# Batch 0 of an attention and FFN kernel: values loaded before queries, queries in two pairs, buffer clearing moved

## Chip, cores, metric

One core of one Trainium2 chip. The metric is the device time of the whole kernel in microseconds (us), median of several runs. "Span" in the profile is some 1.8 to 1.9 us shorter than this time (259.6 against 261.4 for the profiled run of the kernel before), because it runs from the first to the last instruction.

## The reference, cut

```python
# attention: batch 8, heads 8, sequence 576, head size 64
r   = maximum(x, 0);  phi(x) = concat(r * cos_w, r * sin_w)    # 64 -> 128 features, weights by position
kv  = einsum('bhsf,bhsd->bhfd', phi(k), v);   z = sum(phi(k), axis=2)
x   = einsum('bhsf,bhfd->bhsd', phi(q), kv) / (phi(q) . z + 1e-6)
# FFN on x as 4608 tokens of 512
out = ((x @ w1) * (x @ w2)) @ w3 @ w_out       # the kernel multiplies w3 @ w_out once
```

## The kernel before

The tokens go through the FFN in nine tiles of 512. The attention of later batches is spread in "slots" between the FFN products. Only batch 0 has nothing to hide behind: its attention is a prologue. These are its parts (cuts marked).

```python
    load_first(nc.sync, k0, k)              # keys, fp32, 1 MB, on the SyncE queue
    load_first4(nc.sync, k0, k)
    load_first(nc.gpsimd, q0, q)            # queries, 512 KB as bf16, GpSimd queue
    ...
    idle_mms(34)                            # products of zeros: keep TensorE's clock up
    cosv, sinv = _trig_tables(nc, const)    # position table, on VectorE
    load_first(nc.gpsimd, v0, v)            # values
    load_first4(nc.gpsimd, v0, v)
    make_identity(nc, identb[:])
    for i in range(2):                      # two sets of feature buffers
        ... memset ones column of va, and the unused half of va, kp, qp (chunk 4)
    ... loads of w1, w2, wout, w3, batch 1 and 2, all on the GpSimd queue

    def features(b, dst, src, c):           # cosine half on VectorE, sine half on ScalarE
    def kv_first():                         # key-value products: heads 0-3 over all chunks, then 4-7
    def q_tr(b, c):                         # 8 transposes of query features, copied to qpT
    def num(b, c):                          # 8 products, then on VectorE: den, reciprocal, xblk
    def x_tr(b, c):                         # 4 transposes of xblk, copied to xT on ScalarE

    # the prologue
    for c in range(NCH): prep_k(0, c)
    for c in range(4):   prep_q(0, c)
    for c in range(3):   q_tr(0, c)
    idle_mms(1)
    for c in range(NCH): prep_v(0, c)
    q_tr(0, 3, evac=False)[1]()             # copied by ScalarE
    kv_first()
    idle_mms(1); num(0, 0); num(0, 1); idle_mms(3); num(0, 2); x_tr(0, 0)
    idle_mms(2); num(0, 3); x_tr(0, 1)
    first.close()                           # its PSUM banks become the FFN accumulators
    ps_ffn = ...
    # tile 0: the first products in quarters of 128 tokens; x_tr(0, 2), x_tr(0, 3) in slots 0 and 1
            for quarter in range(4):
                for i in range(4):
                    products(acc[i], (w1b, w2b)[i % 2], i // 2, ts(quarter, 128))
                    ...
                yield
```

Of the kernel before, what the change touches and what calls it, by code (L numbers as in the profile page):

```python
# [10 lines left out]
FP32 = mybir.dt.float32  # L11
BF16 = mybir.dt.bfloat16
I32 = mybir.dt.int32
ALU = mybir.AluOpType
ACTF = mybir.ActivationFunctionType

P = 128
H, S, D = 8, 576, 64
F = 2 * D
NCH = 5  # L20
# [48 lines left out]
def kernel(  # L69
# [11 lines left out]
    nc = tc.nc  # L81
# [32 lines left out]
                                in_=src[b, :, 320:S, :].rearrange("h (p j) d -> p h (j d)", j=4))  # L114
            raw[b, name] = t

    def load_first(eng, t, src):
        eng.dma_start(out=t[:, :, 0:4, :].rearrange("p h j d -> p h (j d)"),  # L118
                      in_=src[0, :, 0:512, :].rearrange("h (p j) d -> p h (j d)", j=4))

    def load_first4(eng, t, src):
        eng.dma_start(out=t[0:64, :, 4, :], in_=src[0, :, 512:S, :].rearrange("h p d -> p h d"))
# [14 lines left out]
    v0 = raw[0, "v"] = ld.tile([P, H, NCH, D], BF16, name="vs")  # L137
    load_first(nc.sync, k0, k)
    load_first4(nc.sync, k0, k)
    load_first(nc.gpsimd, q0, q)  # L140
    zeros = const.tile([P, 512], BF16, name="zeros")
    nc.vector.memset(zeros[:], 0.0)
    tiny = const.tile([P, 1], FP32, name="tiny")
    nc.scalar.activation(out=tiny[:], in_=zeros[:, 0:1], func=ACTF.Relu, scale=1.0, bias=0.0)

    unread = ps_first.tile([P, 512], FP32, name="unread")

    def idle_mms(n):

        for _ in range(n):  # L150
            nc.tensor.matmul(unread[:, :], lhsT=zeros[:, 0:128], rhs=zeros[:], start=True, stop=True)

    idle_mms(34)
    cosv, sinv = _trig_tables(nc, const)
    identb = const.tile([P, P], BF16, name="identb")
    load_first(nc.gpsimd, v0, v)
    load_first4(nc.gpsimd, v0, v)
    make_identity(nc, identb[:])

    va_bufs, kp_bufs, qp_bufs = [], [], []  # L160
    for i in range(2):
        va = const.tile([P, NCH, H, D + 2], BF16, name=f"va{i}")
        nc.vector.memset(va[:, :, :, D:D + 1], 1.0)
        nc.vector.memset(va[64:128, 4, :, 0:D], 0.0)
        va_bufs.append(va)
        for name, bufs in (("kp", kp_bufs), ("qp", qp_bufs)):
            fp = const.tile([P, NCH, H, F], BF16, name=f"{name}{i}")
            nc.vector.memset(fp[64:128, 4, :, :], 0.0)  # L168
            bufs.append(fp)
    for c0, n in ((0, 256), (256, 256), (512, 512)):  # L170
        nc.gpsimd.dma_start(out=w1b[:, :, ds(c0, n)], in_=w1v[:, :, ds(c0, n)])
        nc.gpsimd.dma_start(out=w2b[:, :, ds(c0, n)], in_=w2v[:, :, ds(c0, n)])
        if c0 == 0:
            load_first4(nc.gpsimd, q0, q)
# [69 lines left out]
    def prep_q(b, c):  # L244
        features(b, feat_of(b)[1], raw[b, "q"], c)
        if c in dma_q(b):
            R = ROWS[c]
            nc.sync.dma_start_transpose(out=att_of(b)["qpT"][:, :, ds(columns_of(b, c), R)],
                                        in_=feat[b][1][:R, c].rearrange("p h f -> p (h f)"))
# [21 lines left out]
    def kv_first():  # L271

        kp, qp, va = feat[0]
        kvs = sm.tile([P, H, D + 1], BF16, name="kvs", bufs=2)
        kva = ps_first.tile([P, 512], FP32, name="kva")
        kvb = ps_att.tile([P, 2, 512], FP32, name="pnum")
        for half, kvt in enumerate((kva[:, :], kvb[:, 0, :])):
            for c in range(NCH):
                for i in range(4):
                    nc.tensor.matmul(kvt[:, ds(i * 65, 65)], lhsT=kp[:, c, 4 * half + i, :],  # L280
                                     rhs=va[:, c, 4 * half + i, 0:D + 1],
                                     start=(c == 0 and i == 0), stop=(c == NCH - 1 and i == 3))
            dst, src = kvs[:, 4 * half:4 * half + 4, :], kvt[:, 0:260]
            if half == 0:
                nc.scalar.copy(out=dst, in_=src)
            else:
                nc.vector.tensor_copy(out=dst, in_=src)
        att_of(0)["kvs"] = kvs

    def q_tr(b, c, evac=True):  # L290
        R = ROWS[c]
        qp = feat[b][1]
        pst = ps_tr.tile([P, 8, 128], BF16, name="pst")
        for h in range(H):
            nc.tensor.transpose(pst[:, h, :], qp[:, c, h, :], identb[:])  # L295
        dst, src = att_of(b)["qpT"][:, :, ds(columns_of(b, c), R)], pst[:, :, 0:R]
        on_vector = lambda: nc.vector.tensor_copy(out=dst, in_=src)  # L297
        on_scalar = lambda: nc.scalar.copy(out=dst, in_=src)
        if evac:
            on_vector()  # L300
        return on_vector, on_scalar
# [81 lines left out]
    def ffn_groups(t):  # L383
        x = xT[t]
        abT = fsb.tile([P, 8, 512], BF16, name="abT", bufs=2)

        def products(out_ps, w, jc, tok):
            for kc in range(4):
                nc.tensor.matmul(out_ps[:, tok], lhsT=w[:, kc, ts(jc, 128)], rhs=x[:, kc, tok],  # L389
                                 start=(kc == 0), stop=(kc == 3))  # L390

        def to_abT(jc, aT, bT):
            asb = fsb.tile([P, 512], BF16, name="asb")
            nc.scalar.copy(out=asb[:], in_=aT[:, :])
            nc.vector.tensor_mul(out=abT[:, jc, :], in0=asb[:], in1=bT[:, :])

        if t == 0:
            acc = [ps_ffn.tile([P, 512], FP32, name="ffnps") for _ in range(4)]
            for quarter in range(4):
                for i in range(4):  # L400
                    products(acc[i], (w1b, w2b)[i % 2], i // 2, ts(quarter, 128))
                    if i % 2 == 1 and quarter == 3:
                        to_abT(i // 2, acc[i - 1], acc[i])
                yield
        for jc in range(2 if t == 0 else 0, 8):
            aT = ps_ffn.tile([P, 512], FP32, name="ffnps")
            products(aT, w1b, jc, slice(0, 512))
            asb = fsb.tile([P, 512], BF16, name="asb")
            nc.scalar.copy(out=asb[:], in_=aT[:, :])  # L409
            yield  # L410
            bT = ps_ffn.tile([P, 512], FP32, name="ffnps")
            products(bT, w2b, jc, slice(0, 512))
            nc.vector.tensor_mul(out=abT[:, jc, :], in0=asb[:], in1=bT[:, :])  # L413
            yield
        for ms in range(3 if t == NT - 1 else 4):
            ops = ps_ffn.tile([P, 512], FP32, name="ffnps")
            for jc in range(8):
                nc.tensor.matmul(ops[:, :], lhsT=abT[:, jc, ts(ms, 128)], rhs=w34b[:, jc, :],  # L418
                                 start=(jc == 0), stop=(jc == 7))
                if jc == 3:  # L420
                    yield
            if ms % 2 == 0:
                osb = fsb.tile([P, 2, 512], FP32, name="osb", bufs=2)
            nc.scalar.copy(out=osb[:, ms % 2, :], in_=ops[:, :])  # L424
            if t == NT - 1:
                store(nc.sync, osb[:, ms % 2:ms % 2 + 1, :], 4 * t + ms, 1)
            elif ms % 2 == 1:
                store(nc.gpsimd, osb[:, :, :], 4 * t + ms - 1, 2)
            yield
        if t == NT - 1:  # L430
            for half in range(2):
                cols = ts(half, 256)
                ops = ps_ffn.tile([P, 512], FP32, name="ffnps")
                for jc in range(8):
                    nc.tensor.matmul(ops[:, 0:256], lhsT=abT[:, jc, ts(3, 128)],
                                     rhs=w34b[:, jc, cols], start=(jc == 0), stop=(jc == 7))
                nc.scalar.copy(out=osb[:, 1, cols], in_=ops[:, 0:256])
                store((nc.sync, nc.scalar), osb[:, 1:2, :], 4 * t + 3, 1, cols)
                yield
# [9 lines left out]

    for c in range(NCH):  # L450
        prep_k(0, c)
    for c in range(4):
        prep_q(0, c)
    for c in range(3):
        q_tr(0, c)
    idle_mms(1)
    for c in range(NCH):
        prep_v(0, c)
    q_tr(0, 3, evac=False)[1]()
    kv_first()  # L460
    idle_mms(1)
    num(0, 0)
    num(0, 1)
    idle_mms(3)
    num(0, 2)
    x_tr(0, 0)
    idle_mms(2)
    num(0, 3)
    x_tr(0, 1)
    first.close()  # L470
    ps_ffn = ctx.enter_context(tc.tile_pool(name="ps_ffn", bufs=4, space=bass.MemoryType.PSUM))

    for t in range(NT):
        slots = [[] for _ in range(24)]
        if t == 0:
            slots[0].append(lambda: x_tr(0, 2))
            slots[1].append(lambda: x_tr(0, 3))
            slots[1].append(lambda: prep_q(0, 4))
# [63 lines left out]
```

## Time and profile before

| | kernel before |
|---|---|
| time, median (lowest to highest of 3 runs) | 261.54 us (261.39 to 261.55) |
| granted TensorE clock, mean | 0.998 |
| first FFN product (first of w1, 128 columns) | 21.29 us |
| first full FFN product (512 columns) | 25.52 us |
| last products of the kernel start | 253.18 us |

The three marks are read from the timeline of TensorE and from the chain of waits. They cut the span into the prologue, the quarter products of tile 0, and the rest. In the rest TensorE is dense, so it should always last the same: 253.18 - 25.52 = 227.66 us. If a kernel shows more there, a new wait has come up. In profile lines, PE is TensorE, PEld its weight loads, DVE VectorE, ACT ScalarE and POOL GpSimd. The tiles are kf, qs and vs (keys, queries and values as loaded), kp and qp (their features), va (values as copied for the products), kva and pnum (key-value products and numerators, in PSUM, the memory that TensorE writes), kvs (the former, copied), qpT (transposed query features), xblk (a normalised block, 128 rows of attention output) and xT (its transpose). L numbers are lines of that kernel's own source, "A<-B" means that A is written from B, and "[4.94 <-DMA kf]" that the engine sat idle 4.94 us until DMA finished kf.

### The profile page before, as it was taken

How to read it: one execution, taken by the hardware profiler on the slowest of the kernel's cores; microseconds unless marked ns; L12 is line 12 of the kernel's file. 1: busy time of each engine (PE TensorE's matmuls, PEld its weight loads, DVE VectorE, ACT ScalarE, POOL GpSimd, SP SyncE). 2: the span in 40 equal slices, each digit the busy share in tenths (PEclk: the TensorE clock that was granted, in tenths of full speed). 3: DMA queues.
4: the chain of work that ended last, by engine and by line, in shares of the span. 5: the costliest groups of instructions: out<-in, count | busy, mean ns of one | idle time of the engine just before them, and what ended most of it. 6: DMA issues, size and time to landing. Idle time of an engine off the chain costs nothing.

```text
span 259.6 us, 5067 instructions
## 1 busy us (share of the span) xinstructions
PE 250.6 (97%) x1961; PEld 134.9 (52%) x1961; DVE 147.2 (57%) x345; ACT 127.2 (49%) x218; POOL 83.3 (32%) x143
## 2 busy tenths in 40 slices
PE   8789999999999999999999999999999999999992
PEld 2367455666555556445544654464455444444442
DVE  5975656478699627844873587178616613413310
ACT  2826327637955554654655555645533233323322
POOL 7462245340591276047404910520050031012000
PEclk9999999999999999999999999999999999999999
DMA  7999999999399889977998999825590252014015
GB/s 192 188 196 207 210 200 204 199 199 195 96 180 174 145 184 179 196 134 153 190 166 182 155 197 129 184 81 107 107 202 13 40 115 90 0 32 132 1 42 121
DMA packets 65928, 37.10 MB, mean 143 GB/s; under 512 B 33520, under 2 KB 62448, under 8 KB 65904
## 3 DMA queue, kind: packets, MB, share of 16 engines
q0 software_dynamic: 33392, 27.20, 63.7%
q1 hardware_dynamic: 32352, 9.44, 20.2%
q8 instruction: 15, 0.25, 0.4%
q10 hardware_dynamic: 160, 0.13, 0.2%
q14 instruction: 9, 0.07, 0.1%
HBM read 38.80 MB, written 9.44 MB: 186 GB/s over the span
## 4 chain that ended last, share of the span: by engine, by line
PE 90%; DVE 5%; issue 1%; POOL 1%; ACT 1%; ACTq 0%; POOLq 0%
PE ffnps L389 48%; PE ffnps L418 23%; PE ffnps L205 5%; PE pst L295 4%; PE pnum L313 4%; PE pnum L262 3%; PE pst L193 1%; DVE kp L236 1%; DVE xblk L320 1%; PE pst L342 1%; DVE qpT L297 1%; PE kva L280 0%; DVE qp L236 0%; POOL qs L118 0%; DVE qp L168 0%
## 5 line engine op out<-in xcount | busy, mean ns | idle before, releaser
L413 DVE TENSOR_TENSOR abT<-asb,ffnps 128x512 bf16<-128x512 bf16 x70 | 47.8, 683 | 69.3 <-PE ffnps L389 66.7
L389 PE MATMUL ffnps<-xT,w1b 128*128 128x512 bf16 (+1 forms) x312 | 74.9, 362 | 0.5 <-DVE den L317 0.5
L389 PE MATMUL ffnps<-xT,w2b 128*128 128x512 bf16 (+1 forms) x312 | 74.9, 362 | 0.0
L409 ACT CAST asb<-ffnps 128x512 bf16<-128x512 f32 x70 | 41.0, 586 | 64.9 <-PE ffnps L389 57.9
L418 PE MATMUL ffnps<-w34b,abT 128*128 128x512 bf16 x280 | 63.7, 379 | 0.0
L381 POOL DMA_DIRECT2D out_dram<-osb x42 | 22.3, 537 | 122.4 <-ACT osb L424 122.3
L389 PEld LDWEIGHTS <-w1b 128*128 128x128 bf16 x312 | 28.0, 98 | 28.2 <-issue 0.8
L418 PEld LDWEIGHTS <-abT 128*128 128x128 bf16 x280 | 26.7, 98 | 30.2
L389 PEld LDWEIGHTS <-w2b 128*128 128x128 bf16 x312 | 26.9, 98 | 23.9
L424 ACT COPY osb<-ffnps 128x512 f32<-128x512 f32 x35 | 20.5, 585 | 36.6 <-PE ffnps L418 36.6
L238 ACT ACTIVATE qp<-qs,sinv 128x512 bf16<-128x512 bf16 (+1 forms) x40 | 28.2, 721 | 0.0
L320 DVE TENSOR_TENSOR xblk<-pnum,den 128x512 bf16<-128x512 f32 (+1 forms) x38 | 26.3, 691 | 1.3
L238 ACT ACTIVATE kp<-ks,sinv 128x512 bf16<-128x512 bf16 (+1 forms) x35 | 24.7, 722 | 0.0
L313 PEld LDWEIGHTS <-qpT 128*128 128x128 bf16 x320 | 15.1, 98 | 9.3 <-DVE xblk L320 1.5
L254 POOL COPY va<-vs 128x512 bf16<-128x512 bf16 (+1 forms) x30 | 18.6, 644 | 0.0
L236 DVE TENSOR_SCALAR qp<-qs,cosv 128x512 bf16<-128x512 bf16 (+1 forms) x40 | 18.1, 468 | 0.0
L297 DVE COPY qpT<-pst 128x1024 bf16<-128x1024 bf16 (+1 forms) x23 | 14.4, 628 | 4.7 <-PE pst L295 4.2
L295 PEld LDWEIGHTS <-qp 128*128 128x128 bf16 x192 | 12.5, 98 | 7.2 <-ACT qp L238 1.9
L295 PE MATMUL pst<-identb,qp 128*128 128x128 bf16 x192 | 14.5, 219 | 1.8 <-DVE qp L236 1.4
L313 PE MATMUL pnum<-kvs,qpT 128*128 128x65 bf16 x304 | 16.0, 194 | 0.0
L205 PE MATMUL ffnps<-woutb,w3T 128*128 128x512 bf16 x64 | 15.8, 379 | 0.0
L262 PEld LDWEIGHTS <-kp 128*128 128x128 bf16 x280 | 12.9, 98 | 5.4
(73 smaller groups left out, 174.7 us busy)
## 6 DMA issues: line engine op xcount, KB each, us to landing
out_dram<-osb POOLq DMA_DIRECT2D x16, 256.0 KB, 3.9
out_dram<-osb POOLq DMA_DIRECT2D x24, 128.0 KB, 3.0
ks<-in_k_dram POOLq DMA_DIRECT2D x7, 320.0 KB, 5.9
vs<-in_v_dram POOLq DMA_DIRECT2D x7, 320.0 KB, 8.0
qs<-in_q_dram POOLq DMA_DIRECT2D x7, 320.0 KB, 6.5
w3b<-in_moe_w_dram POOLq DMA_DIRECT2D x8, 256.0 KB, 15.0
ks<-in_k_dram POOLq DMA_DIRECT2D x7, 256.0 KB, 6.7
vs<-in_v_dram POOLq DMA_DIRECT2D x7, 256.0 KB, 9.7
```

Source lines behind the costliest of these rows:

```text
L205: nc.tensor.matmul(acc[:, :], lhsT=w3T[:, lc, :], rhs=woutb[:, lc, :], start=(lc == 0), stop=(lc == 7))
L236: nc.vector.tensor_scalar(out=dst[:R, c, :, 0:D], in0=src[:R, :, c, :], scalar1=0.0, scalar2=cosv[:R, at:at + 1], op0=ALU.max, op1=ALU.mult)
L238: nc.scalar.activation(out=dst[:R, c, :, D:F], in_=src[:R, :, c, :], func=ACTF.Relu, scale=sinv[:R, at:at + 1], bias=0.0)
L262: nc.tensor.matmul(kvt[:, h // 4, ds((h % 4) * 65, 65)], lhsT=kp[:, c, h, :], rhs=va[:, c, h, 0:D + 1], start=(i == 0 and h % 4 == 0), sto ...
L295: nc.tensor.transpose(pst[:, h, :], qp[:, c, h, :], identb[:])
L313: nc.tensor.matmul(nt[:, h // 4, ds((h % 4) * 65, 65)], lhsT=qpT[:, h, ds(at, 128)], rhs=kvs[:, h, :], start=True, stop=True)
L320: nc.vector.tensor_tensor(out=xblk[rows], in0=n4[:, :, :, 0:D], in1=den[rows].unsqueeze(3).to_broadcast([R, 2, 4, D]), op=ALU.mult)
L381: on.dma_start(out=rows[:, :, cols], in_=osb[64 * i:64 * i + rows.shape[0], :, cols])
L389: nc.tensor.matmul(out_ps[:, tok], lhsT=w[:, kc, ts(jc, 128)], rhs=x[:, kc, tok], start=(kc == 0), stop=(kc == 3))
L409: nc.scalar.copy(out=asb[:], in_=aT[:, :])
L413: nc.vector.tensor_mul(out=abT[:, jc, :], in0=asb[:], in1=bT[:, :])
L418: nc.tensor.matmul(ops[:, :], lhsT=abT[:, jc, ts(ms, 128)], rhs=w34b[:, jc, :], start=(jc == 0), stop=(jc == 7))
```

## The change

The intent: clear the buffers when VectorE has nothing to do, compute the key-value products while the queries are still in flight, split the queries so that the first two chunks go ahead, and put the fourth numerator among the first FFN products.

```diff
-    def load_first(eng, t, src):
+    def load_first(eng, t, src, c0=0, n=4):          # chunks c0 to c0+n
...
-    load_first(nc.gpsimd, q0, q)
+    load_first(nc.gpsimd, v0, v)
     zeros = ...; nc.vector.memset(zeros[:], 0.0)
+    def feature_buffers(i): ...                       # the clearing, as before
+    feature_buffers(0)
...
-    idle_mms(34)
+    idle_mms(28)
     cosv, sinv = _trig_tables(nc, const)
-    load_first(nc.gpsimd, v0, v)
     load_first4(nc.gpsimd, v0, v)
+    load_first(nc.gpsimd, q0, q, 0, 2)
     make_identity(nc, identb[:])
-    for i in range(2): ...                            # the clearing of both sets
+    load_first(nc.gpsimd, q0, q, 2, 2)
...                                                    # kv_first: all heads of a chunk, chunk by chunk
     for c in range(NCH): prep_k(0, c)
-    for c in range(4): prep_q(0, c)
-    for c in range(3): q_tr(0, c)
-    idle_mms(1)
     for c in range(NCH): prep_v(0, c)
-    q_tr(0, 3, evac=False)[1]()
     kv_first()
+    for c in range(2): prep_q(0, c)
+    idle_mms(2); q_tr(0, 0); q_tr(0, 1)
+    for c in range(2, 4): prep_q(0, c)
     idle_mms(1)
     num(0, 0)
+    q_tr(0, 2, evac=False)[1]()
+    idle_mms(1)
+    q_tr3 = q_tr(0, 3, evac=False)[1]
     num(0, 1)
-    idle_mms(3); num(0, 2); x_tr(0, 0); idle_mms(2); num(0, 3); x_tr(0, 1)
+    idle_mms(2); x_tr(0, 0); q_tr3(); num(0, 2); x_tr(0, 1)
+    feature_buffers(1)
     first.close()
...
-            for quarter in range(4): ...
+            for group in (((0, 0),), ((0, 1), (1, 0)), ((1, 1), (0, 2), (1, 2)), ((0, 3), (1, 3))):
...
         if t == 0:
+            slots[0].append(lambda: num(0, 3))
```

More of the change, by code (lines that the diff above doesn't have):

```diff
@@ L115, in load @@
             raw[b, name] = t
-    def load_first(eng, t, src):
-        eng.dma_start(out=t[:, :, 0:4, :].rearrange("p h j d -> p h (j d)"),
-                      in_=src[0, :, 0:512, :].rearrange("h (p j) d -> p h (j d)", j=4))
+    def load_first(eng, t, src, c0=0, n=4):
+        rows = src[0, :, 0:512, :].rearrange("h (p j) d -> p h j d", j=4)
+        eng.dma_start(out=t[:, :, c0:c0 + n, :].rearrange("p h j d -> p h (j d)"),
+                      in_=rows[:, :, c0:c0 + n, :].rearrange("p h j d -> p h (j d)"))
     def load_first4(eng, t, src):
@@ L139, with feature_buffers @@
     load_first4(nc.sync, k0, k)
-    load_first(nc.gpsimd, q0, q)
+    load_first(nc.gpsimd, v0, v)
     zeros = const.tile([P, 512], BF16, name="zeros")
     nc.vector.memset(zeros[:], 0.0)
-    tiny = const.tile([P, 1], FP32, name="tiny")
-    nc.scalar.activation(out=tiny[:], in_=zeros[:, 0:1], func=ACTF.Relu, scale=1.0, bias=0.0)
-    unread = ps_first.tile([P, 512], FP32, name="unread")
-    def idle_mms(n):
-        for _ in range(n):
-            nc.tensor.matmul(unread[:, :], lhsT=zeros[:, 0:128], rhs=zeros[:], start=True, stop=True)
-    idle_mms(34)
-    cosv, sinv = _trig_tables(nc, const)
-    identb = const.tile([P, P], BF16, name="identb")
-    load_first(nc.gpsimd, v0, v)
-    load_first4(nc.gpsimd, v0, v)
-    make_identity(nc, identb[:])
     va_bufs, kp_bufs, qp_bufs = [], [], []
-    for i in range(2):
+    def feature_buffers(i):
         va = const.tile([P, NCH, H, D + 2], BF16, name=f"va{i}")
@@ L169, with idle_mms @@
             bufs.append(fp)
+    feature_buffers(0)
+    tiny = const.tile([P, 1], FP32, name="tiny")
+    nc.scalar.activation(out=tiny[:], in_=zeros[:, 0:1], func=ACTF.Relu, scale=1.0, bias=0.0)
+    unread = ps_first.tile([P, 512], FP32, name="unread")
+    kva = ps_first.tile([P, 512], FP32, name="kva")
+    def idle_mms(n):
+        for _ in range(n):
+            nc.tensor.matmul(unread[:, :], lhsT=zeros[:, 0:128], rhs=zeros[:], start=True, stop=True)
+    idle_mms(28)
+    cosv, sinv = _trig_tables(nc, const)
+    identb = const.tile([P, P], BF16, name="identb")
+    load_first4(nc.gpsimd, v0, v)
+    load_first(nc.gpsimd, q0, q, 0, 2)
+    make_identity(nc, identb[:])
+    load_first(nc.gpsimd, q0, q, 2, 2)
     for c0, n in ((0, 256), (256, 256), (512, 512)):
@@ L274, in kv_first @@
         kvs = sm.tile([P, H, D + 1], BF16, name="kvs", bufs=2)
-        kva = ps_first.tile([P, 512], FP32, name="kva")
         kvb = ps_att.tile([P, 2, 512], FP32, name="pnum")
-        for half, kvt in enumerate((kva[:, :], kvb[:, 0, :])):
-            for c in range(NCH):
-                for i in range(4):
-                    nc.tensor.matmul(kvt[:, ds(i * 65, 65)], lhsT=kp[:, c, 4 * half + i, :],
-                                     rhs=va[:, c, 4 * half + i, 0:D + 1],
-                                     start=(c == 0 and i == 0), stop=(c == NCH - 1 and i == 3))
-            dst, src = kvs[:, 4 * half:4 * half + 4, :], kvt[:, 0:260]
-            if half == 0:
-                nc.scalar.copy(out=dst, in_=src)
-            else:
-                nc.vector.tensor_copy(out=dst, in_=src)
+        halves = (kva[:, :], kvb[:, 0, :])
+        for c in range(NCH):
+            for h in range(H):
+                nc.tensor.matmul(halves[h // 4][:, ds((h % 4) * 65, 65)], lhsT=kp[:, c, h, :],
+                                 rhs=va[:, c, h, 0:D + 1], start=(c == 0 and h % 4 == 0),
+                                 stop=(c == NCH - 1 and h % 4 == 3))
+        nc.scalar.copy(out=kvs[:, 0:4, :], in_=halves[0][:, 0:260])
+        nc.vector.tensor_copy(out=kvs[:, 4:8, :], in_=halves[1][:, 0:260])
         att_of(0)["kvs"] = kvs
@@ L398, in ffn_groups @@
             acc = [ps_ffn.tile([P, 512], FP32, name="ffnps") for _ in range(4)]
-            for quarter in range(4):
-                for i in range(4):
-                    products(acc[i], (w1b, w2b)[i % 2], i // 2, ts(quarter, 128))
-                    if i % 2 == 1 and quarter == 3:
-                        to_abT(i // 2, acc[i - 1], acc[i])
+            for group in (((0, 0),), ((0, 1), (1, 0)), ((1, 1), (0, 2), (1, 2)), ((0, 3), (1, 3))):
+                for jc, quarter in group:
+                    products(acc[2 * jc], w1b, jc, ts(quarter, 128))
+                    products(acc[2 * jc + 1], w2b, jc, ts(quarter, 128))
+                    if quarter == 3:
+                        to_abT(jc, acc[2 * jc], acc[2 * jc + 1])
                 yield
@@ L451 @@
         prep_k(0, c)
-    for c in range(4):
-        prep_q(0, c)
-    for c in range(3):
-        q_tr(0, c)
-    idle_mms(1)
     for c in range(NCH):
         prep_v(0, c)
-    q_tr(0, 3, evac=False)[1]()
     kv_first()
+    for c in range(2):
+        prep_q(0, c)
+    idle_mms(2)
+    q_tr(0, 0)
+    q_tr(0, 1)
+    for c in range(2, 4):
+        prep_q(0, c)
     idle_mms(1)
     num(0, 0)
+    q_tr(0, 2, evac=False)[1]()
+    idle_mms(1)
+    q_tr3 = q_tr(0, 3, evac=False)[1]
     num(0, 1)
-    idle_mms(3)
+    idle_mms(2)
+    x_tr(0, 0)
+    q_tr3()
     num(0, 2)
-    x_tr(0, 0)
-    idle_mms(2)
-    num(0, 3)
     x_tr(0, 1)
+    feature_buffers(1)
     first.close()
```

## The prediction

> **What bounds the kernel now.** I read the views in this order: the busy time of each engine in stretches of the span, the chain of work that ended last, the timeline of the first 28 us, and the DMA issues with their times to landing.
>
> The stretches say that there are two regimes.
>
> ```profile
> core 0: us, PE busy (x) PEld busy (x) DVE busy (x) ACT busy (x) POOL busy (x), PEclk, DMA share, GB/s
> 0.00:11.00 11.00, 9.78 (x34) 3.80 (x34) 7.17 (x27) 5.31 (x9) 8.37 (x19) 1.00 1.07 190
> 11.00:21.30 10.30, 7.28 (x120) 5.52 (x121) 8.56 (x27) 4.21 (x7) 4.49 (x7) 1.00 1.46 196
> 21.30:32.00 10.70, 10.62 (x117) 7.29 (x118) 5.58 (x12) 4.80 (x10) 2.62 (x4) 1.00 1.20 209
> ...
> 60.00:235.00 175.00, 175.00 (x1333) 91.93 (x1331) 103.59 (x236) 91.82 (x158) 55.37 (x94) 1.00 0.78 134
> ```
>
> The reader is to see the first number after the comma. From 21.3 us on TensorE is busy without a gap (10.62 of 10.70, then 175.00 of 175.00), and the change does not touch the work there apart from its first 5 us. Before 21.3 us its 34 early matmuls are multiplications of zeros, and VectorE is the engine that is nearly full (8.56 of 10.30). So only the prologue can give time, and what it gives must survive 200 us of dense TensorE work: the start of the dense work moves the end one for one, unless a load becomes late.
>
> The chain of waits names the path through the prologue.
>
> ```profile
> 9.80 2.19 DVE kp L236 x5
> 11.99 1.05 DVE qp L236 x4
> ...
> 13.04 0.70 DVE qpT L297
> ...
> 15.12 0.21 DVE va L254
> ...
> 15.38 1.09 PE kva L280 x20
> 16.46 0.65 PE pnum L280 x20
> ...
> 20.46 0.69 DVE xblk L320
> 21.15 0.08 DVE den L317
> 21.23 0.06 issue
> 21.29 1.05 PE ffnps L389 x16
> ```
>
> It is VectorE almost throughout. The first FFN product at 21.29 waits until the third normalised block (20.46 + 0.69 = 21.15) has been read out of its PSUM banks, because the FFN accumulators take those banks.
>
> ```profile
> 7.17 3.17 ACT L238 ACTIVATE kp<-kf,sinv 128x512 bf16<-128x512 f32 x5 [4.94 <-DMA kf<-in_k_dram]
> 8.76 0.48 DVE L168 MEMSET kp<- 64x512 uint32 x1
> 9.80 2.19 DVE L236 TENSOR_SCALAR kp<-kf,cosv 128x512 bf16<-128x512 f32 x5
> 10.03 0.96 POOL L171 DMA_DIRECT2D w1b<-in_moe_w_dram  x1 [1.27 <-DMA qs<-in_q_dram]
> 12.97 0.74 POOL L172 DMA_DIRECT2D w2b<-in_moe_w_dram  x1 [1.98 <-DMA vs<-in_v_dram]
> 15.09 1.01 ACT L298 COPY qpT<-pst 128x1024 bf16<-128x1024 bf16 x1 [2.30 <-PE pst L295]
> ```
>
> In this timeline the keys are there at 7.17 (ScalarE starts), yet VectorE starts on them only at 9.80: it is clearing buffers from 6.52 to 9.79. The bracketed releasers give the loads: the first 512 KB on the GpSimd queue (queries) has landed by 10.03, the second (values) by 12.97; by issue plus time to landing they are 9.8 and 12.7, and the 64 KB of values after them 13.2.
>
> **What the Trainium skill says.** First, "DMA: Bandwidth & Descriptors", section Specifications, puts the least transfer for line rate at 512 B. The split query load has pieces of 512 B in memory and 256 B on chip, against 1 KB and 512 B. The trace only partly agrees that small pieces hurt: 64 KB of values in 256 B source pieces took 13.2 - 12.7 = 0.5 us for 512 pieces, while 512 KB took about 2.9 us for 1024 pieces of 1 KB, so bytes count more than pieces. Second, "TensorE: Matmul & The Clock Gate", section "Wait — 56ns, not 53.3ns?", has warm matmuls of 128 columns 55.6 ns apart; 16 of L389 take 0.89 us in the chain, 55.6 ns each, so it agrees. Third, "VectorE: DVE Perf Modes", section "Why PSUM operands drop a tier", explains why reading PSUM stays slow: the normalisation of 512 elements takes 0.69 us here and no reordering shortens it.
>
> **The change part by part.**
>
> *Memsets.* The first buffer set is cleared while VectorE waits for the position table (idle 1.81 us before 2.95); its four memsets take about 1.5 us (6.52 to 8.06), so the table still starts near 2.95 and ends near 6.4. The second set goes behind the third normalised block. VectorE can start the keys at about 7.2 and end at 7.2 + 2.2 = 9.4. Worth 9.80 - 7.2 = 2.6 us, if what follows is there.
>
> *Values first.* They take the queries' place and land at 9.8 to 10.0, their last chunk by 10.5. Copies to the value buffer: 10.0 to 11.1 (1.08 for five). The 40 key-value products follow chunk by chunk; the last 20 in the trace took 0.65, 33 ns each, so eight take 0.26 against 0.21 for a copy: from 10.3 to about 11.7. Both halves are then copied at once, 0.43, to 12.2. Before, this was 17.57.
>
> *Queries in two pairs.* Two points give a line: 512 pieces of 256 B in 0.5 us, 512 of 1 KB in 1.45; so 512 of 512 B about 0.85, a pair of chunks (1024 pieces) 1.7. They land at about 12.2 and 13.9 (estimate). VectorE makes the cosine features of the first pair 12.2 to 12.75; ScalarE, at 0.635 each, 12.2 to 13.5, and of the second pair 13.9 to 15.2. The first transpose starts at 12.9; from its start to the copy was 0.64 (12.40 to 13.04), so the two copies of qpT (0.69 each) run 13.5 to 14.9, then cosine features of the second pair to 15.45. First normalisation (0.18 + 0.21 + 0.69 with gaps is 1.08): 15.45 to 16.5. Transposes of chunks 2 and 3: 15.2 to 16.3; second numerator to 16.7; second normalisation 16.75 to 17.8. Now ScalarE copies chunk 2 of qpT (1.01) 15.85 to 16.85, the first xT (0.59) 17.3 to 17.9, chunk 3 17.9 to 18.9. Third numerator 17.2 to 17.6, third normalisation 17.8 to 18.85. First FFN product: **18.9**, against 21.29, so 2.4 us earlier.
>
> *What is paid back.* In the order of the built program the first FFN product still waits for the third normalised block, so the reordering does not lift that wait. The fourth numerator, done before the FFN until now, comes inside it: 0.45. Its normalisation stands behind the second set of memsets, 1.55, so block four is ready at 18.85 + 1.55 + 1.08 = 21.45. TensorE meanwhile does eight products (0.45), numerator (0.45), a transpose (0.22), sixteen products (0.9): it reaches the fourth transpose at 20.95 and stalls 0.5. Then 0.22, 24 products (1.35), 16 products (0.9): ends at 24.0. Before, the 64 quarter products ended at 25.26. Gain 25.26 - 24.0 = **1.25 us**.
>
> *Zero products.* 28 instead of 34 at the start, four fewer later: none on the path; the 28 end at 10.98 - 6 x 0.215 = 9.7, before the values.
>
> *Downstream.* Loads do not come earlier when TensorE does. Issue plus time to landing: second part of batch 1's queries 46.7, first used about 47.45; its values 42.3, used 43.8; weights w3 block 6 47.6, used 49.76. A shift of 1.25 turns only the queries into a wait, of about 0.5, on ScalarE, which idles over 1 us soon after (49.28); TensorE needs them at 51.06. So all 1.25 us reach the end: 261.5 - 1.25 = 260.2, 0.5%.
>
> **The rivals.** (1) Pieces set the query load: at 2.9 us a pair as for 1024 pieces now, the pairs land at 13.3 and 16.2, ScalarE ends features at 17.5, the third block moves to 20.8 and the gain becomes a loss of about 0.7: 262.2. Against it stands the 0.5 us of the 256 B pieces. (2) ScalarE sets the end instead of VectorE: it alternates between 1.01 copies of qpT and xT copies, and the fourth numerator needs the last one (18.9 above, just in time). With 0.5 us of slip there: 260.7. (3) The stall behind the memsets is hidden, because TensorE arrives later than I reckon or numerators slip: no stall, 259.7. (4) Sparser TensorE work from 9.7 to 19 lets its clock drop; the granted clock is 1.00 through the old gaps of 1.4 us, and I count about 7 us of work in 9.2, as dense as before. If it drops, half a microsecond to one is lost. (5) Batch 1's loads, pushed by the longer query load, bind at 45 to 50 us and cap the gain near 1 us.
>
> **Range and chances.** Centre 260.2. Half a microsecond either way comes from the stall and ScalarE, the tail upward from rival 1: 259.2 to 261.4 eight times in ten. Faster by over 2% would need 5.2 us, over twice the whole advance at the first FFN product; slower by over 2% would need the loads to come 7 us late. Chances: faster 0.01, same 0.98, slower 0.01.
>
> **What would show it.** In the changed timeline: keys on VectorE at about 7.2; values copied from about 10.0; kvs by 12.2; first pair of query features released by its load near 12.2, second near 13.9; first FFN product near 18.9, released by the third block; an idle of about 0.5 on TensorE before the fourth transpose, released by the fourth block; quarter products over by 24.0; no new idle of TensorE after. I am wrong if the second pair lands after 15, if the first FFN product is later than 20, or if TensorE shows waits between 35 and 60 us.

## The result, and the profile after

The changed kernel takes 259.91 us (259.70 to 260.16, 4 runs) against 261.48 (4 runs) of the kernel before. The ratio is 0.9941, 95% interval 0.9923 to 0.9958. All runs are fast (none is over 1.5% above the fastest of its kernel). A ratio here is the mean time of one kernel's fast runs over the mean of the other's in the same rounds, so it is not quite the ratio of the medians quoted.

Busy time by stretch, kernel after, the same columns as in the prediction:

```profile
11.00:21.30 10.30, 7.47 (x117) 5.73 (x114) 8.54 (x24) 6.49 (x10) 4.63 (x8) 1.00 1.47 197
21.30:32.00 10.70, 10.62 (x97) 6.38 (x96) 4.88 (x10) 5.00 (x9) 2.62 (x4) 1.00 1.20 208
...
60.00:235.00 175.00, 175.00 (x1327) 91.62 (x1326) 102.81 (x234) 91.29 (x157) 56.45 (x96) 1.00 0.79 137
```

The dense regime is unchanged: 175.00 of 175.00, and the same clock. What moved is how early it begins. The chain of waits of the kernel after:

```profile
1.28 8.12 DMA vs<-in_v_dram
...
9.43 0.31 DVE va L260
...
11.15 0.38 ACT kvs L288
11.53 0.63 ACT qp L244
...
12.86 1.30 DVE qpT L299 x2
...
17.61 0.69 DVE xblk L322
...
19.44 0.48 DVE qp L154
...
20.40 0.70 DVE xblk L322
21.10 0.05 issue
21.15 0.40 PE pst L344 x4
```

Read it from the top. The chain no longer starts on VectorE but with the load of the values. From there it goes through the value copies, the first query feature on ScalarE and the query copies to the third block (17.61). Then comes what is new: the clearing of the second set (19.44 is its last piece) and the fourth block, on which the fourth transpose waits. The timeline has the same with the idle times:

```profile
6.76 2.29 DVE L242 TENSOR_SCALAR kp<-kf,cosv 128x512 bf16<-128x512 f32 x5 [0.56 <-DMA kf<-in_k_dram]
11.56 0.74 POOL L178 DMA_DIRECT2D w2b<-in_moe_w_dram  x1 [0.39 <-DMA qs<-in_q_dram]
12.98 0.88 POOL L181 DMA_DIRECT2D woutb<-in_moe_w_out_dram  x1 [0.68 <-DMA qs<-in_q_dram]
18.45 0.38 PE L391 MATMUL ffnps<-xT,w1b 128*128 128x128 bf16 x4 [0.64 <-DVE xblk L322]
21.15 0.40 PE L344 MATMUL pst<-identb,xblk 128*128 128x128 bf16 x4 [0.72 <-DVE xblk L322]
```

VectorE now waits for the keys (0.56 us) where it was clearing buffers before. The first pair of queries has landed by 11.56 and the second by 12.98. TensorE stalls 0.72 us at 21.15.

The three marks of every kernel, each from its profiled run:

| kernel | median us | ratio to before | first FFN product | to first full product | from there to the last products |
|---|---|---|---|---|---|
| before | 261.4 to 261.5 | 1 | 21.29 | 4.23 | 227.66 |
| after | 259.91 | 0.9941 | 18.45 | 5.38 | 227.66 |
| after, once more | 260.08 | 0.9944 | 18.70 | 5.38 | 227.66 |
| clearing moved, nothing else | 260.35 | 0.9958 | 20.35 | 4.22 | 227.66 |
| all but the clearing | 262.24 | 1.0032 | 21.65 | 4.76 | 227.67 |
| the same, 42 zero products | 261.99 | 1.0026 | 21.44 | 4.76 | 227.67 |
| the same, 39 zero products | 261.49 | 0.9998 | 21.03 | 4.77 | 227.67 |
| queries whole | 261.10 | 0.9984 | 19.65 | 5.38 | 227.65 |
| second set cleared before the keys | 259.79 | 0.9939 | 19.21 | 4.76 | 227.67 |
| second set cleared in slot 5 | 259.89 | 0.9944 | 18.60 | 4.77 | 228.28 |
| old quarter order | 259.58 | 0.9929 | 18.84 | 4.94 | 227.64 |
| second set cleared in slot 10 | 259.49 | 0.9925 | 18.81 | 4.77 | 227.76 |
| combined | 259.56 | 0.9929 | 18.45 | 4.76 | 228.19 |
| combined, w3 block ahead | 260.41 | 0.9956 | 18.69 | 4.77 | 228.86 |

The change gains 21.29 - 18.45 = 2.84 us up to the first FFN product, gives 5.38 - 4.23 = 1.15 back in the quarter products, and nothing after: 1.69 us between the profiled runs. The two right-hand columns repeat to 0.02 us where the code is the same, so they are the ones to compare.

The first mark does not repeat so well. Five of these kernels have the prologue of the change unaltered up to this mark (after, once more, slot 5, slot 10, old quarter order), and their first mark lies between 18.45 and 18.84; the profiled run of the change is the fastest of its four. The spread begins where the key-value products start, at 9.78 to 10.14. They need three things that come within half a microsecond of each other, and each came last in one of these runs: the copied values in the changed kernel (their load landed at 9.40), ScalarE's half of the key features in the slot 10 run (until 10.10), and the end of the 28 zero products in the run with the old quarter order (10.07). Zero products start 0.43 us apart at first and 0.22 apart later. The switch came between 3.7 and 7.0 us, differently from run to run, and the clock column shows 1.00 all the while (its record begins only about there). So a number of zero products does not fix when they end.

### The profile page after: what moved, and what is told of

Its sections match the earlier page's. It is cut to its first block, busy times and chain, and to the rows that moved or that the text cites. A ratio compares the mean times of both kernels' runs of the same rounds, so it can differ in the third digit from the quotient of the medians.

```text
span 257.9 us, 5056 instructions
## 1 busy us (share of the span) xinstructions
PE 248.3 (96%) x1954; PEld 134.0 (52%) x1954; DVE 147.0 (57%) x344; ACT 128.3 (50%) x219; POOL 84.3 (33%) x144
## 2 busy tenths in 40 slices
DMA packets 66968, 37.10 MB, mean 144 GB/s; under 512 B 35584, under 2 KB 63488, under 8 KB 66944
## 4 chain that ended last, share of the span: by engine, by line
PE 91%; DMA 3%; DVE 2%; ACT 1%; issue 1%; ACTq 0%; POOLq 0%
PE ffnps L391 47%; PE ffnps L421 23%; PE ffnps L211 5%; PE pst L297 4%; PE pnum L315 4%; PE pnum L268 3%; DMA vs<-in_v_dram 3%; PE pst L199 1%; DVE xblk L322 1%; PE pst L344 1%; DVE qpT L299 1%; PE ffnps L438 0%; PE kva L285 0%; ACT osb L440 0%; DVE den L320 0%
## 5 line engine op out<-in xcount | busy, mean ns | idle before, releaser
L391 PEld LDWEIGHTS <-w2b 128*128 128x128 bf16 x312 | 26.9, 97 | 23.9
L299 DVE COPY qpT<-pst 128x1024 bf16<-128x1024 bf16 (+1 forms) x22 | 13.7, 626 | 5.0 <-PE pst L297 4.7
```

The lines of the kernel that those rows point to most:

```text
L391: nc.tensor.matmul(out_ps[:, tok], lhsT=w[:, kc, ts(jc, 128)], rhs=x[:, kc, tok], start=(kc == 0), stop=(kc == 3))
```

## The experiments

All kernels gave correct results. All but the first start from the changed kernel; all were run in five rounds with the kernel before.

### 1. The clearing alone

```diff
 # kernel before
+    feature_buffers(0)                  # after the memset of zeros
...
-    for i in range(2): ...              # both sets, between position table and keys
...
     x_tr(0, 1)
+    feature_buffers(1)                  # behind the fourth block
     first.close()
```

> The kernel before with nothing but the buffer clearing moved: first set while VectorE waits for the position table, second set behind the fourth normalised block. Loads, order of work and quarter products as before. My working: keys on VectorE at 7.2 instead of 9.8, query features held by their load at 9.8, the transposed-query copies 11.6 to 13.7, the value copies 13.7 to 14.8 instead of 15.0 to 16.1 (values land at 13.2), so 1.3 us earlier from there on, 260.2. Rival A (the clearing is the whole of the change, the load order adds nothing): as the changed kernel, 259.9. Rival B (the value load at 12.7 to 13.2 holds the old order, so early keys give nothing): 261.3 or more.

Measured 260.35 us, ratio 0.9958 (0.9945 to 0.9970). The first FFN product comes at 20.35, 0.94 us earlier; nothing is given back. Neither rival holds: the clearing alone brings 1.0 us, about two thirds of the change's gain. It lies 0.15 above my number. The value copies ran from 13.64 as reckoned, but took 1.53 us instead of 1.08, because the second of the five took 0.73 and the others 0.28; why it did is not shown.

### 2. All but the clearing

```diff
-    feature_buffers(0)
...
     make_identity(nc, identb[:])
+    for i in range(2): feature_buffers(i)      # as in the kernel before
...
-    feature_buffers(1)
```

> The changed kernel with both sets cleared where the kernel before cleared them, ahead of the keys; loads, order and quarter products stay changed. My working: keys end at about 12, value copies 12 to 13.1 although the values landed at 9.4, the first FFN product 2.4 us later than in the changed kernel (20.9), but the stall before the fourth transpose (0.7) goes: 1.7 us slower than the changed kernel, 261.6, that is, no gain over before. Rival A (the new load order carries the gain): 260.3 or less. If the two parts simply added up to the change's 1.6 us, this run would give 261.4 less whatever the clearing alone does not give.

Measured 262.24 us, ratio 1.0032 (1.0019 to 1.0044): slower than before, and 0.6 above my number. The stall is gone as expected (4.76 in the second column). Two lines of the stretches and one of the timeline show where the 0.6 went:

```profile
11.00:12.00 1.00, 0.00 (x0) 0.00 (x0) 1.00 (x3) 0.00 (x0) 0.79 (x2) 0.77 1.84 183
12.00:13.00 1.00, 0.84 (x16) 0.84 (x16) 1.00 (x5) 0.00 (x0) 0.81 (x1) 0.50 1.56 193
```

```profile
12.16 0.38 PE L286 MATMUL kva<-va,kp 128*128 128x65 bf16 x4 [3.03 <-DVE va L261]
```

The 28 zero products end at 9.1, the values are copied only from 11.84, and TensorE sits idle for 3.03 us. Its granted clock (third number from the right) falls to 0.50, and the 40 key-value products take 2.1 us instead of about 1.35. So this run tested the loads and a slow clock together. The next two take them apart.

### 3. The same with 42, then 39 zero products

```diff
-    idle_mms(28)
+    idle_mms(42)      # then 39
```

> The run with the loads and order of the change and the old clearing, but 42 instead of 28 zero products at the start, so that TensorE works until about 12.1 and its clock is not lowered (it was 0.50 from 12 to 14.5 us, and the 40 key-value products took 2.2 us instead of 1.35). My theory: the clock cost 0.8 us of that run, so 261.4 to 261.5, equal to the kernel before. Rival (the lowered clock was off the path, VectorE is the path): 262.2 as in that run.

Measured 261.99 us, ratio 1.0026 (1.0013 to 1.0038). The clock stayed at 1.00, but the zero products ran to 12.80 and held the key-value products although the first values were copied by about 12.15. The first line is from the run with 28 of them, the second from this one:

```profile
1.20 7.94 PE L166 MATMUL unread<-zeros 128*128 128x512 bf16 x28 [1.20 <-DVE zeros L143]
...
1.20 11.77 PE L166 MATMUL unread<-zeros 128*128 128x512 bf16 x42 [1.20 <-DVE zeros L143]
```

The count was not wrong: 14 more at 0.216 us should have added 3.0 us, not 3.8. Their slow start lasted until 6.3 us here and until 4.6 in the run with 28. The run is inconclusive on size.

> The run with loads and order alone, with 39 zero products: 42 overran and held the key-value products until 12.80 although the values were ready at 12.15, so that run tested two things at once. With 39 they should end at about 12.15 and the products run warm from 12.2. My theory: the lowered clock cost 0.8 of that kernel, 261.4, level with the kernel before. Rival: 262.0 to 262.2.

Measured 261.49 us, ratio 0.9998 (0.9986 to 1.0010). This time the slow start was short, and the zero products ended before the values came:

```profile
12.39 0.29 PE L286 MATMUL kva<-va,kp 128*128 128x65 bf16 x4 [1.08 <-DVE va L261]
```

With a clock of 1.00 throughout, the new load order, the pairs and the new order of work gain nothing that shows above the noise over the kernel before, as my theory had it: the first FFN product is 0.26 earlier, and the quarter phase, which now holds the fourth numerator, 0.54 longer. The lowered clock had cost 0.62 us by the first FFN products of the two profiled runs (21.65 against 21.03) and 0.75 by the medians (262.24 against 261.49; the two were run in different rounds; their ratios differ by 0.0034, or 0.9 us).

Together with experiment 1 this gives a square: clearing alone -1.0, the rest alone 0.0 (with 39 zero products, so that the clock stays up), both -1.5. The parts do not add. The runs show that; the reason that follows is read from the timelines. With the old clearing the values wait for VectorE, which is busy with the keys until about 11.8, so early values are of no use. With the old load order the value copies stand behind the query copies. Only both together let the values be the next thing when VectorE comes free.

### 4. Queries in one load

```diff
-    load_first(nc.gpsimd, q0, q, 0, 2)
+    load_first(nc.gpsimd, q0, q)
     make_identity(nc, identb[:])
-    load_first(nc.gpsimd, q0, q, 2, 2)
```

> The changed kernel with batch 0's queries in one load of 512 KB behind the values. My theory: they land at about 12.7, when the second pair now lands; ScalarE's four feature instructions then run from 12.7 instead of 11.4, and everything behind them is 1.2 us later: 261.1, so most of the change's gain is gone. Rival A (ScalarE and VectorE are filled by other work, the pairs are cosmetic): 259.9. Rival B (the split's small pieces cost the queue more than the early half gives): below 259.9.

Measured 261.10 us, ratio 0.9984 (0.9972 to 0.9997). The timeline has ScalarE waiting for the load:

```profile
12.63 2.56 ACT L243 ACTIVATE qp<-qs,sinv 128x512 bf16<-128x512 bf16 x4 [0.72 <-DMA qs<-in_q_dram]
```

In the changed kernel these four instructions begin at 11.43, so they are 1.2 us later here. The load accounts for 0.72 of that. The other 0.5 was there before: the values landed at 9.79 instead of 9.40 in this execution, within what runs with the split show too (up to 9.86), and the key-value products started 0.38 later. By the medians the whole load costs 1.0 to 1.2 us (against 260.08 and 259.91). So the split is worth 0.7 to 1.2 us of the change's 1.5 once the rest is in place, and rivals A and B both fall.

### 5. The second set cleared before the keys

```diff
     make_identity(nc, identb[:])
+    feature_buffers(1)
...
-    feature_buffers(1)
```

> The changed kernel with only the second set cleared where both sets were cleared before, between the position table and the keys. My theory: the keys start about 1 us later (7.8 instead of 6.8) and end at 10.1, so the values, landed at 9.4 to 9.8, are copied 0.3 to 0.6 late; in return the stall of 0.7 before the fourth transpose goes. The two cancel: 259.8, within 0.2 of the changed kernel. Rival (moving the second set off the keys is what the change lives on): 260.5 or more.

Measured 259.79 us, ratio 0.9939 (0.9923 to 0.9955), level with the change. The first FFN product is 0.76 later than in the changed kernel's profiled run and the quarter phase 0.62 shorter: the two cancel. So moving the second set to where the change has it gains nothing; moving the first set does (both sets ahead of the keys: 261.49 in experiment 3). A side finding: five of the six runs lie between 259.77 and 259.79 (one at 260.86), while the changed kernel spreads over half a microsecond (259.70 to 260.16, then 259.91 to 260.42). Here VectorE works on the keys until 10.3, later than the values land (9.4) and later than the zero products end (9.2), so that neither can move the key-value products. In the changed kernel both can. Which of them makes the spread is not separated.

### 6. The second set cleared in slot 5, then in slot 10

```diff
-    feature_buffers(1)
...
+            slots[5].append(lambda: feature_buffers(1))     # then slots[10]
```

> The changed kernel with the second set cleared after the first FFN products of tile 0 (fifth slot) instead of ahead of the fourth normalisation. My theory: the stall of 0.72 us before the fourth transpose shrinks to under 0.1 and all of it reaches the end: 259.2 to 259.3. Rival (the stall is hidden by something behind it, such as the copies out of PSUM or the second pair of weights): within 0.15 of the changed kernel, 259.8. Second rival (1.5 us of clearing in the middle of the FFN delays the products out of PSUM there): slower than 259.9.

Measured 259.89 us, ratio 0.9944 (0.9930 to 0.9957): no gain, and the first rival's number. But the table shows that neither rival names what happened. The quarter phase is shorter by 0.61 (4.77), and the dense part longer by 0.62 (228.28):

```profile
30.07 0.29 PE L344 MATMUL pst<-identb,xblk 64*128 64x64 bf16 x4 [0.66 <-DVE xblk L322]
```

The stall stands before the fifth transpose now: the clearing had come between VectorE and the fifth block. The cost had only moved. The second rival had the kind of thing right (clearing in the middle of the FFN delays VectorE's other work), but the work that waited was the fifth block and not a product out of PSUM.

> The changed kernel with the second set cleared in the tenth slot of tile 0, behind the work of the fifth chunk; in the fifth slot the clearing had only moved the stall (0.7 us, now before the fifth transpose at about 29.5 instead of the fourth). My theory: with nothing of the attention waiting behind the clearing there, neither stall is left and the time is 0.65 to 0.7 below the changed kernel: 259.2. Rival (something else takes the wait, such as the products out of PSUM): 259.8 or more.

Measured 259.49 us, ratio 0.9925 (0.9912 to 0.9937). In slot 10 nothing of the attention waits behind it. The quarter phase is 4.77 and the dense part 227.76. Its first FFN product came at 18.81, 0.1 to 0.4 later than in the two profiled runs of the change, so the gain is 0.4 by the medians, 0.5 by the ratios, and 0.5 in the two right-hand columns together (232.53 against 233.04). The 0.65 that I expected is not quite reached.

### 7. The old quarter order

```diff
-            for group in (((0, 0),), ((0, 1), (1, 0)), ((1, 1), (0, 2), (1, 2)), ((0, 3), (1, 3))):
+            for group in [((0, quarter), (1, quarter)) for quarter in range(4)]:
```

> The changed kernel with the quarter products of tile 0 in the old order, quarter by quarter. My theory: the reordering lifts no wait (the first product still waits for the third block), and the old order gives TensorE 0.45 us more to do ahead of the fourth transpose, so the stall falls from 0.72 to about 0.3 and the time to 259.5. Rival (the reordering is needed: it lets the second and third xT copies come in time): 0.3 us or more slower than the changed kernel, 260.2.

Measured 259.58 us, ratio 0.9929 (0.9916 to 0.9941). The quarter phase is 4.94, 0.44 shorter. The stall before the fourth transpose fell from 0.72 to 0.27 us, as the theory says: TensorE has sixteen products rather than eight before the fourth numerator.

```profile
21.55 0.40 PE L344 MATMUL pst<-identb,xblk 128*128 128x128 bf16 x4 [0.27 <-DVE xblk L322]
```

The reordering in the change costs 0.4 us where it stands; no wait came back without it.

### 8. Combined, and a w3 block ahead

```diff
+            slots[10].append(lambda: feature_buffers(1))     # and the old quarter order
     q_tr(0, 2, evac=False)[1]()
-    idle_mms(1)
     q_tr3 = q_tr(0, 3, evac=False)[1]
```

> The clearing in the tenth slot, the old quarter order, and one zero product taken out between the transposes of chunks 2 and 3, which the chain of waits of the changed kernel shows on its path with 0.22 us. My theory: 0.2 below the run with the clearing in the tenth slot alone, 259.0; the old quarter order adds nothing once the stall is gone. Rival (the first FFN product is held elsewhere, or the clock falls without the zero product): no better than that run, 259.2.

Measured 259.56 us, ratio 0.9929 (0.9915 to 0.9942), no better than slot 10 alone. Up to the first full product it is the fastest of all, 18.45 + 4.76 = 23.21. Without the one zero product, 8.46 us pass from the first key-value product to the first FFN product instead of 8.67; the old quarter order adds nothing once the stall is gone (4.76 against 4.77), both as expected. Then the dense part takes 228.19, 0.53 more than it should:

```profile
47.70 0.45 PEld L199 LDWEIGHTS <-w3b 128*128 128x128 bf16 x8 [0.39 <-DMA w3b<-in_moe_w_dram]
47.71 0.62 PE L199 MATMUL pst<-identb,w3b 128*128 128x128 bf16 x8 [0.26 <-DMA w3b<-in_moe_w_dram]
```

TensorE has caught up with the weight loads. In the kernel before, this block landed at 47.57 and TensorE started on it at 49.59, so it had 2.0 us to spare. The work had moved up by 25.52 - 23.21 = 2.3 us and the block, which landed at 47.66 here, had not. In the run with the clearing in slot 10, 1.94 us ahead, there was no such wait.

```diff
-    load(1, "q"); load_w3(6); load_w3(7)
+    load_w3(6); load(1, "q"); load_w3(7)
```

> The combined run with one w3 block loaded ahead of batch 1's queries. In the combined run TensorE waited 0.7 us in all for that block at about 47.7, so it gave no more than the run with the late clearing although its first FFN product and its first full product came 0.36 earlier. My theory (the loads now bind): that wait goes and the time falls by 0.3 to 0.6, to 259.1. Rival (the wait only moves to the queries of batch 1, which ScalarE and VectorE already wait for by 1.0 and 1.2 us): 259.5 or more.

Measured 260.41 us, ratio 0.9956 (0.9944 to 0.9968): worse, and the rival holds.

```profile
48.02 0.61 DVE L242 TENSOR_SCALAR qp<-qs,cosv 128x512 bf16<-128x512 bf16 x2 [1.43 <-DMA qs<-in_q_dram]
...
51.21 0.61 PE L297 MATMUL pst<-identb,qp 128*128 128x128 bf16 x8 [0.89 <-DVE w3T L201]
```

The wait for w3 became a longer wait for batch 1's queries, and TensorE met it at 51.21 through VectorE. So with this set of loads the prologue has about 1.8 us to give, and no more was reached: the slot 10 and the combined run are 1.94 and 2.31 us ahead of the kernel before at the first full product, and 1.84 and 1.78 at the last products (251.34 and 251.40 against 253.18). The two orders that I tried trade one late block for another. Whether a third order does better is open.

### 9. The change once more

> The changed kernel once more, on the same chip and in the same rounds as these: 259.9, 0.994 of the kernel before. Its runs should again spread over 0.4 us where the kernel before spreads over 0.1, because its chain now starts at a load (the values) and not at VectorE.

Measured 260.08 us, ratio 0.9944 (0.9932 to 0.9955), spread 0.51 us. The kernel before spread over 0.31 in these rounds apart from one run at 262.32, so the comparison of spreads is weaker here than the 0.12 and 0.18 of the earlier rounds suggest. That the load causes the spread is not shown: the end of the zero products moves too (see the marks above), and no run holds one of the two fixed.

## Why the prediction was right

The time (260.2 predicted, 259.91 measured) and most of its steps hold. Rival 3 named a nearer number (259.7), but not what happened: its stall was to vanish, and it is there. Point by point:

- *Keys at 7.2.* At 6.76, released by their load: 0.4 earlier, because the load itself came in earlier (the keys' load took 6.0 us to land instead of 6.3; between 5.5 and 6.4 in the runs here). The reason was right.
- *Values at 9.8 to 10.0, kvs by 12.2.* Copied from 9.43, kvs by 11.7. This is the term that was off: the values landed after 8.1 us where the queries in the same place had taken 8.5. Most later marks carry these 0.4 to 0.5 us: first FFN product 18.45 for 18.9. Part of that is which execution was profiled: the same load took 8.1 to 8.6 us in the other runs, and the same prologue reached 18.84.
- *Query pairs at 12.2 and 13.9.* By issue plus time to landing 11.3 and 12.7. My line through two points (1.7 us a pair) overcharged the smaller pieces: the second pair of 256 KB followed the first by 1.4 us, about the rate per byte of the unsplit load (2.9 for 512 KB). Rival 1 was wrong altogether. The error had little effect: VectorE and ScalarE were busy with kvs until the first pair was needed, and ScalarE's four features ran without a gap from 11.43 to 14.05, where I had 0.4 us of waiting for the second pair.
- *First FFN product still waits for the third block.* Yes (0.64 of idle, released by xblk); experiment 7 shows that the reordering does not lift it and costs 0.4.
- *Stall of 0.5 at the fourth transpose.* 0.72. Quarter phase 18.9 to 24.0, then the first full product 0.26 later as before, is 5.36; measured 5.38. So close an agreement is partly luck: the terms behind the stall (0.22 + 1.35 + 0.9) add to 2.5 and end at 23.9, not 24.0, and that slip made up for part of the stall's extra 0.2. Experiments 5 and 6 show that the clearing causes the stall.
- *Zero products, 28 end at 9.7, none on the path.* They ended at 8.9, and TensorE idled 0.87 us before the key-value products. The working had taken six products fewer at 0.215 off a run whose slow start was longer (until 5.85 us, here 4.16). That they were not on the path was luck of the execution: with the same prologue they held the key-value products in the run of experiment 7.
- *ScalarE (rival 2).* It did not set the end: its last copy of query features ended at 18.29, before the fourth numerator at 18.89. It is on the chain early, with kvs and the first query feature (11.15 to 12.16).
- *Clock.* Stayed at 1.00 in the changed kernel, so rival 4 did not come in; experiments 2 and 3 show that it was a real danger, 0.6 to 0.9 us.
- *Downstream.* ScalarE waited 0.75 for batch 1's queries (0.5 predicted), VectorE also 0.46 for its values, since the shift was 1.69 and not 1.25, and TensorE for nothing. Block 6 of w3 had 2.0 us to spare, not the 2.2 of the prediction: 49.76 is where the chain puts the end of the work before it, and the timeline has its first use at 49.59. Rival 5 (loads cap the gain near 1 us) was right that there is a cap and wrong about where: it showed at about 1.8, at a w3 block.

The prediction's remark that reading PSUM keeps the normalisation at 0.69 us was not tested: no run changes where that operand lies.

What the prediction did not see is that the parts do not add (the square in experiment 3), and that the new quarter order is not neutral but 0.4 us slower than the old one where it stands.

## What to carry to other kernels

Cut the span at a few marks that bound regimes and compare the differences between marks, not only total times: here they repeat to 0.02 us and found a stall that had moved (experiment 6) where the time alone said "no effect". An early load pays only if the engine that takes it is free then, and a free engine only if the data is there; judge such parts together. When work moves up, list the later loads with landing and first use, and by which engine. Batch 1's queries had only 0.75 us to spare, and moving up by 1.69 cost nothing, because ScalarE, which takes them, could wait. The w3 block had 2.0, and TensorE, which has no idle time there, takes it: that was the limit. A number of filler products is no timer: look where they end in several runs.

## What the Trainium skill lacked or had wrong

- "TensorE: Matmul & The Clock Gate", section "What's actually happening", has the clock halved after at least one idle window of about 3.4 us. Here an idle gap of 3.03 us was enough (experiment 2): the granted clock was 0.77 on average from 11 to 12 us and 0.50 from 12 to 14, which for one step from 1.00 to 0.50 puts it at about 11.5, some 2.4 us after the last zero product (an estimate from these means). The halved value agrees; the gaps of 1.4 us of the kernel before left the clock at 1.00.
- "DMA: Bandwidth & Descriptors", section Specifications, asks for 512 B or more for line rate. A query load split into pieces of 512 B in memory and 256 B on chip landed 256 KB in 1.4 us (11.3 to 12.7), about the rate of pieces of twice the size (512 KB in 2.9 us in the kernel before), with 1040 packets more in the whole run (66968 against 65928). The unsplit load of experiment 4 had all queries in at 12.6, the pairs at 12.7. The page does not say which side of a converting load the limit is meant for, and no loss beyond 0.1 us showed here.
